# A new instruction order for a fused attention and bilinear kernel, from a search with three smaller constants in its model

## The chip, the cores and the metric

The kernel runs on one core of a Trainium2 chip. The metric is the device time of one execution in microseconds. A core has five engines with a queue of instructions each: TensorE (PE in the profile, with its weight loads as PEld), VectorE (DVE), ScalarE (ACT), GpSimd (POOL) and SyncE (SP), which here only starts DMA transfers. Matmuls write to PSUM, eight banks of 128 partitions by 512 fp32 values; the other engines read the banks and write to SBUF. Engines are ordered among each other by semaphores alone; inside one engine the order of the program holds.

## The reference

One input `x` of 2048 tokens by 512 feeds two branches, which a gate per token mixes. `A` is a multi-head attention with 32 heads of 16, without a mask; `B` is a bilinear unit of width 1376.

```python
qkv = (x @ wqkv).reshape(B, S, 3, H, Dh).transpose(2, 0, 3, 1, 4)
scores = einsum("bhqd,bhkd->bhqk", q, k) * Dh ** -0.5
a = merge_heads(softmax(scores) @ v) @ wo
b = ((x @ w_gate) * (x @ w_up)) @ w_down
g = sigmoid((x * gate_w).sum(-1))
out = g * a + (1 - g) * b
```

All tensors are bf16.

## The kernel before

**Work.** The tokens are cut into four chunks of 512 queries and 16 tiles of 128 keys; the heads into four blocks of eight, of which four pairs lie side by side on the partitions and two parities follow each other. That makes 32 groups (chunk, block, parity), and a group has 16 x 4 score units: one unit is the scores of one head for 128 keys by 512 queries, one PSUM bank. There are 2,048 units.

**TensorE has two tilings.** In the row tiling the array is four tiles of 32 rows, and one burst computes up to four units, one for each head of the four, each into a bank of its own (`burst`, the matmul in L910). In the column tiling it is four tiles of 32 columns, and one pack of four matmuls adds probabilities times values for four heads into the one output bank (`pv_pack`, L1143), or does one 128-deep piece of a projection, of the bilinear unit or of the output (`mm_col`, L427, called by `run_fill`). A piece of the output tile may also be cut into quarters of 32 rows, one of which rides along in a burst (`mm_row`, L433).

**The exponentials** are shared by two engines. ScalarE takes one, two or three neighbouring banks with one instruction (`act_step`, L1008). VectorE computes a base value for one bank by integer arithmetic on the bits (`dve_exp`, L1043), and GpSimd derives two shifted copies of it (`pool_step`, L1093); three packs with differently scaled values then replace one. `more` gives VectorE 20 or 24 of a group's 64 units. The rest of VectorE's work is the evacuation of projections, the bilinear products, the softmax's denominators and the output.

**What sets the order.** The kernel is planned when it is built. `_Clock` keeps a model time for each engine; `issue` notes when an operation begins, when its engine is free again (`dur`) and when its result can be used (`lat`, and 55 ns more for a semaphore, `SEM`). At each model time every free engine is asked for its next step: `pe_step` lists the candidates (a burst `b`, a burst with other shares `x` or `y`, a burst into banks that are about to be free `l`, a pack `p`, a fill `f`, waiting `w`), `act_step` chooses among three, two and one banks, `dve_step` between an evacuation and an exponential. Wherever there is more than one candidate, `choose` reads the next digit of the string `ORDER` as the index into the list. The string thus fixes the whole program; it has 3,094 digits, one for each such decision, and 2,690 of them are 0, the first candidate. The string is the outcome of a search outside of the kernel, which isn't part of it.

The constants of the model that matter here are `MM` (a pack or burst, 216 ns), `SWITCH` (added where the tiling changes, in `pe_issue`), `SECOND` (added to the step behind), `AHEAD` and `LATER` (how long before a bank is free a step in the other tiling may be planned into it) and the `dur` and `lat` of each instruction. None of them is an operand of an instruction. What the plan emits are the instructions in each engine's order, with semaphore waits for the true dependences alone: a constant that is too short can't break a dependence, it only puts an instruction at a place where it will wait.

Of the kernel before, what the change touches and what calls it, by code (L numbers as in the profile page):

```python
# [203 lines left out]
def bass_gated_mix__mha_block__glu_gated_bilinear__prompt_kernel(  # L204
# [12 lines left out]


ORDER = (
    "0000000000000011000001000001000001000000010001000001000000500000000000000000000000001000001010501000"  # L220
    "0000100000000000000000000010001000010000010000000000100000000000000100001000010200000000200010000003"
    "0000000000000040000100000000002002000000000100101000000100010000011100000000000000000000100001000000"
    "5000000020000000200100000010000000000000010000302000000002000000000020020400000000000000100000010000"
    "2000202000012000000000000000000002100000000001000100000000000000020030010030010000000000000022000020"
    "0001000000000001000000000040000000000002210000000000000030010000000000000000001000011000000001000000"
    "0002100000010000000100040000000100000010100000001000000000200000002020000000010000000000200001010000"
    "1005000000000000010000400000010000000000000003000000000000000030100000000010000010000000000000000010"
    "0300000100000000100000000104000000000000000200000002000000000100000000000000000000000010000100000130"
    "3101004000010000100000000000000000000010020000000000000000000000000103030002000100000010000000000000"
    "0000000000000000021000000013030000000000001000011000002200000001100020000000000000002000000002000000"  # L230
    "0200000000200001000200003000000000000000000000020000001000000000000400010002000000000400000020000000"
    "0000000040000000000020000000200000002001200000000000010000000002002000002000000000000000002020100002"
    "0000000040000000100301000000000000000000000100000310010000000000002000000000000101000000000000000000"
    "0200000002000000000100000050000200000010000000003001000000000003002000000000050000000100020000003000"
    "0000000001000010030000010000010010000000020000000011000000000011000000000000000020002200000012000000"
    "0000100000000011050000004000000010000000000001011000200000000000000001000000000000000000000000000000"
    "0000010000000100000000000000000000002110000000000100000000401020000004001000000010000000000000000000"
    "0000101000020004000100000000000000002000010000000311000100000033000000000020030000001000000000040000"
    "0100000000010000100000000000100200000000101000200000000000000000010100000000000000200001000100000100"
    "4110000002000000005000004001000000010000000000000000300000020000000200000010000000010001100040000000"  # L240
    "0000010000000100000000000001000000000000000020000000200000000010000000001100000000000000000000100020"
    "0000000000000000001000000001001005000000300000000000001000000001000000000001000000000000000000000000"
    "0000020000000010001000000000000000000010000000500000000000000000000000000000000000001000010000000002"
    "0000000001000000002000200000002000000000000300000011000100000000000000000200020000020000000000000000"
    "0000000000000202000030000010050010300000001000000000020001000000000000000100002000000000000000000002"
    "0000000200000002001000000001000000010000000000000000011020000010000010000000000000001000000000020100"
    "0000200000000000000000101000000000001000000000001000000000000000200200100000002000000020000001000000"
    "0000010000020001000000010001003000000200000001100000000004000000000000000000000000000100000000000000"
    "0020020000000000000000000000000010000220000000000000000000000020000001200000200000000200500000000100"
    "0000000100050000001040001000300001004010020002011002020000200110000000000000000000000000000000"  # L250
)
HOOK, STOP = None, [1e9]
S, D, H, Dh, F = 2048, 512, 32, 16, 1376
# [6 lines left out]
VR = (203 / 256, 161 / 256)  # L260
NC, NPOOL = 58, 7
OB = 7
MM, SWITCH, SECOND, MML, AHEAD, LATER = 216.0, 108.0, 10.0, 390.0, 90.0, 150.0


class _Tile:
# [23 lines left out]
def _build(nc, A_x, A_wqkv, A_wo, W_gate, W_up, W_down, gate_w, out):  # L290
# [8 lines left out]
    with ExitStack() as stack:  # L299
# [479 lines left out]
        pt_free, pt_rel = list(range(NC)), {i: [] for i in range(NC)}  # L779
        pt_rel[0] = pt_first  # L780
        y_out = [0]
        pool_add = deque()
# [190 lines left out]
        def span2(lo, n, step):  # L973
            return slice(lo, lo + (n - 1) * step + 1, step)

        def act_step():
            if K.pick("act", 1):
                return True
            n = min(len(act_ready), len(pt_free) - 2 * y_out[0])
            if n < 0:  # L980
                n = 0
            if not n:
                return K.pick("act")
            us = [act_ready[0]]
            if n > 1:
                near = [x for x in act_ready if abs(x[1] - us[0][1]) == 1]
                at = {x[1] - us[0][1]: x for x in act_ready}
                three = next(([at[a], at[b]] for a, b in ((1, 2), (1, -1), (-1, -2)) if a in at and b in at), None) if n > 2 and len(pt_free) - 2 * y_out[0] >= 10 else None
                how = choose("a", (["3"] if three else []) + ["2", "1"]) if near else "1"
                if how == "3":  # L990
                    us += three
                elif how == "2":
                    us.append(three[0] if three else near[0])
                us.sort(key=lambda x: x[1])
            n = len(us)
            for x in us:
                act_ready.remove(x)
            if n == 3:
                cells = next([a, b, c_] for k1, b in enumerate(pt_free) for a in pt_free for c_ in (2 * b - a,) if a < b and c_ in pt_free)
                for q in cells:  # L1000
                    pt_free.remove(q)
            else:
                cells = sorted(pt_free.pop(0) for _ in range(n))
            banks = [x[1] for x in us]
            deps = [x[2] for x in us] + [o for q in cells for o in pt_rel[q]]
            bs = slice(banks[0], banks[0] + n)
            cs = span2(cells[0], n, cells[1] - cells[0] if n > 1 else 1)
            o = K.issue("act", lambda a: a.activation(PT[:, cs, :], ps[:, bs, :], ACT.Exp, scale=math.log(2.0) / 1024.0),  # L1008
                        deps, 63.0 + 427.0 * n, 176.0 + 427.0 * n)
            soon(o, banks)  # L1010
            act_out[0] -= n
            o.work = 452.0 * n
            for (u, bank, _), q in zip(us, cells):
                m, kt, j = u

                def free(last, q=q):
                    pt_rel[q] = [last]
                    pt_free.append(q)
                put(_PV(m, j, kt, 0, PT[:, q, :], o, free))
            return True  # L1020

        def put(it):
            pvq.setdefault((it.m, it.j), []).append(it)
# [12 lines left out]
        def dve_exp():  # L1036
            if not can_dve():
                return False
            u, bank, dep = dve_ready.popleft()
            by_dve.add(u)  # L1040
            y = pt_free.pop(0)
            y_out[0] += 1
            o = K.issue("dve", lambda v: v.tensor_scalar(PT[:, y, :].bitcast(I16), ps[:, bank, :], BIAS16, 0.0, ALU.add, ALU.max),  # L1043
                        [dep] + pt_rel[y], 600.0, 690.0, lambda o: pool_add.append((u, y, o)))
            soon(o, [bank])
            dve_out[0] -= 1
            o.work = 452.0
            m, kt, j = u
            used = []

            def free(last):
                used.append(last)
                if len(used) == 2:
                    pt_rel[y] = used
                    pt_free.append(y)
            put(_PV(m, j, kt, 0, PT[:, y, :].bitcast(F16), o, free))
            frees[y] = free
            return True
# [402 lines left out]
        def choose(kind, opt):  # L1461

            if len(opt) == 1:
                return opt[0]
            if HOOK is not None:
                return HOOK(kind, opt, K)
            i = n_choice[0]
            n_choice[0] += 1
            return opt[int(ORDER[i])] if i < len(ORDER) and int(ORDER[i]) < len(opt) else opt[0]
# [169 lines left out]
```

## Time and profile before

| | us |
|---|---|
| median of 3 runs | 647.2 |
| lowest and highest | 646.39, 649.96 |
| profiled execution | 646.02 |
| its span, first to last instruction | 644.1 |
| granted TensorE clock, share of full | 0.999 |

The profiled execution's time is 1.9 us longer than the span of its instructions. In the profile's groups a row reads: line, engine, operation, output and inputs, shapes, count, then the busy time in us and the mean of one instruction in ns, then the engine's idle time ahead of the group and what ended it. The busy time of a group is the union of its instructions' time, so four matmuls that run side by side count once. The rows themselves stand in the prediction.

| group | instructions | busy us |
|---|---|---|
| ScalarE's exponentials, L1008 | 743 | 615.5 |
| VectorE's exponentials, L1043 | 728 | 471.9 |
| GpSimd's copies, L1093 | 1,420 | 550.5 |

### The profile page before, as it was taken

The numbers are of one execution on the slowest core, as the hardware profiler recorded it, in microseconds if no ns is written. First come the engines' busy times: TensorE is split into PE (matmuls) and PEld (weight loads), VectorE is DVE, ScalarE is ACT, GpSimd is POOL, SyncE is SP. The second block draws the span as 40 slices with busy tenths as digits, with TensorE's granted clock in tenths as the row PEclk, the third lists the DMA queues.
The fourth block names the chain that finished last, engine by engine and source line by source line (L and its number), as shares of the span: only waits on it lengthen the run. The fifth ranks groups of instructions, "written<-read, shape, count | busy, mean of one in ns | idle before, by whom it ended". The sixth has DMA issues, their size and how long they took to land.

```text
span 644.1 us, 21192 instructions
## 1 busy us (share of the span) xinstructions
PE 636.3 (99%) x8729; PEld 191.4 (30%) x8729; DVE 602.0 (93%) x1020; ACT 621.8 (97%) x754; POOL 553.4 (86%) x1431
## 2 busy tenths in 40 slices
PE   8999999999999999999999999999999999999997
PEld 3332322222223222223232222332322222222333
DVE  6999999999999999999998999999998999999985
ACT  5899999999999999999999999999999999999992
POOL 2669899999999999898889999888897999889881
PEclk9999999999999999999999999999999999999999
DMA  7940201000010100101010010100001010000001
GB/s 151 262 126 16 66 10 40 2 15 24 5 34 10 40 14 16 32 1 36 4 31 16 16 40 11 32 7 21 19 6 40 19 35 3 9 23 1 28 20 36
DMA packets 28659, 21.16 MB, mean 33 GB/s; under 512 B 16488, under 2 KB 24396, under 8 KB 28560
## 3 DMA queue, kind: packets, MB, share of 16 engines
q1 hardware_dynamic: 27744, 19.40, 11.5%
q8 instruction: 68, 1.11, 0.7%
q10 hardware_dynamic: 816, 0.39, 0.2%
q14 instruction: 31, 0.25, 0.2%
HBM read 11.63 MB, written 2.37 MB: 22 GB/s over the span
## 4 chain that ended last, share of the span: by engine, by line
PE 89%; ACT 9%; DMA 1%; SPq 0%; issue 0%
PE ps L1143 32%; PE ps L427 28%; PE ps L910 26%; ACT PT L1008 9%; PE ps L433 3%; DMA wq<-in_A_wqkv_dram 1%; ACT QE L712 0%; PE ps L1254 0%; SPq L354 0%
## 5 line engine op out<-in xcount | busy, mean ns | idle before, releaser
L1008 ACT ACTIVATE PT<-ps 128x1024 bf16<-128x1024 f32 (+2 forms) x743 | 615.5, 1007 | 5.1 <-PE ps L910 4.5
L1093 POOL INT64_ADD PT<-PT x1420 | 550.5, 408 | 74.6 <-DVE PT L1043 65.2
L1043 DVE TENSOR_SCALAR PT<-ps 128x512 int16<-128x512 f32 x728 | 471.9, 683 | 27.2 <-PE ps L910 15.5
L910 PE MATMUL ps<-QE,KK 32*128 32x512 bf16 x2048 | 244.7, 384 | 0.1
L1143 PE MATMUL ps<-PT,V 128*32 128x512 bf16 (+1 forms) x2048 | 232.5, 384 | 0.0
L1143 PE MATMUL ps<-PT,VS 128*32 128x512 f16 x1456 | 186.6, 383 | 0.0
L910 PEld LDWEIGHTS ps<-QE,KK 32*128 32x128 bf16 x2048 | 63.4, 91 | 229.9 <-ACT PT L1008 185.4
L1143 PEld LDWEIGHTS ps<-PT,V 128*32 128x32 bf16 x2048 | 57.7, 95 | 62.9 <-issue 49.4
L1143 PEld LDWEIGHTS ps<-PT,VS 128*32 128x32 bf16 x1456 | 45.5, 95 | 42.0 <-issue 27.0
L427 PE MATMUL ps<-xT,wg 128*32 128x512 bf16 x704 | 54.6, 383 | 0.0
L427 PE MATMUL ps<-xT,wu 128*32 128x512 bf16 x704 | 54.1, 383 | 0.0
L427 PE MATMUL ps<-wd,wa 128*32 128x512 bf16 x704 | 51.6, 382 | 0.0
L624 DVE TENSOR_TENSOR usb<-ps,omg 128x512 bf16<-128x512 f32 x44 | 30.0, 681 | 0.2
L651 DVE TENSOR_TENSOR wa<-ps,usb 128x512 bf16<-128x512 f32 x44 | 29.9, 680 | 0.1
L433 PE MATMUL ps<-wo,OT 32*128 32x512 bf16 x60 | 23.1, 384 | 0.2
L1240 DVE COPY oc<-ps 128x512 f32<-128x512 f32 x31 | 21.1, 680 | 0.0
L427 PEld LDWEIGHTS ps<-wd,wa 128*32 128x32 bf16 x704 | 14.8, 95 | 19.5 <-issue 11.9
L427 PE MATMUL ps<-xT,wa 128*32 128x512 bf16 x272 | 20.2, 382 | 0.0
L427 PE MATMUL ps<-xT,wq 128*32 128x512 bf16 x256 | 18.5, 382 | 1.4 <-DMA wq<-in_A_wqkv_dram 1.4
L427 PEld LDWEIGHTS ps<-xT,wg 128*32 128x32 bf16 x704 | 13.9, 95 | 18.6 <-issue 11.1
L427 PEld LDWEIGHTS ps<-xT,wu 128*32 128x32 bf16 x704 | 13.7, 95 | 19.0 <-issue 10.4
L427 PE MATMUL ps<-wa,xT 128*32 128x512 bf16 x256 | 17.1, 381 | 0.0
(73 smaller groups left out, 140.9 us busy)
## 6 DMA issues: line engine op xcount, KB each, us to landing
rb<-rscr SPq DMA_DIRECT2D x16, 256.0 KB
QE<-Qr SPq DMA_DIRECT2D x120, 16.0 KB, 1.8
oc<-oc SPq DMA_DIRECT2D x60, 32.0 KB, 1.9
out_dram<-ost SPq DMA_DIRECT2D x12, 128.0 KB, 1.7
wu<-in_B_w_up_dram SPq DMA_DIRECT2D x1, 1376.0 KB, 7.1
wg<-in_B_w_gate_dram SPq DMA_DIRECT2D x1, 1376.0 KB, 11.5
wd<-in_B_w_down_dram SPq DMA_DIRECT2D x1, 1280.0 KB, 14.8
wa<-in_A_wqkv_dram SPq DMA_DIRECT2D x1, 512.0 KB, 5.7
```

The costliest lines, as they stand in the source:

```text
L427: r = pe.matmul(ps[32 * i : 32 * i + 32, bank, :], w, x_, start=s0, stop=s1, tile_position=(0, 32 * i), skip_group_check=True)
L433: return pe.matmul(ps[:, bank, :], lhs[32 * q : 32 * q + 32, :], rhs[32 * q : 32 * q + 32, :], start=s0, stop=s1, tile_position=(32 * q, 0 ...
L624: return v.tensor_tensor(usb[:, st["s"], :], ps[:, bank, :], omg[:, cf, :], ALU.mult)
L651: return v.tensor_tensor(hT[:, f, :], ps[:, bank, :], usb[:, u_at[cf, f][0], :], ALU.mult)
L910: return lambda pe: pe.matmul(ps[:, bank, :], KK[32 * j : 32 * j + 32, b, kt * 128 : (kt + 1) * 128], QE[32 * j : 32 * j + 32, p, b, :], s ...
L1008: o = K.issue("act", lambda a: a.activation(PT[:, cs, :], ps[:, bs, :], ACT.Exp, scale=math.log(2.0) / 1024.0), deps, 63.0 + 427.0 * n, 17 ...
L1043: o = K.issue("dve", lambda v: v.tensor_scalar(PT[:, y, :].bitcast(I16), ps[:, bank, :], BIAS16, 0.0, ALU.add, ALU.max), [dep] + pt_rel[y] ...
L1093: return g.int64_add(PT[:, zl, :].bitcast(I64), PT[:, sl, :].bitcast(I64), w)
L1143: return lambda pe: pe.matmul(ps[32 * it.j : 32 * it.j + 32, OB, :], lhs, it.rhs, start=s0, stop=s1, tile_position=(0, 32 * it.j), skip_gr ...
L1240: K.task("dve", deps, lambda v: v.tensor_copy(oc[:, p, :], ps[:, OB, :]), 600.0, 690.0, done, 0)
```

## The change

Three constants of the planner's model become smaller: the cost of a tiling change from 108 to 106 ns, the delay of a ScalarE exponential from 176 + 427 n to 170 + 427 n ns (n banks), and the delay of a VectorE exponential from 690 to 684 ns. `ORDER` is replaced by another string, found by the search with these constants and another seed. It has 3,108 digits, of which 2,695 are 0, and differs from the first digits on. No function gets other code.

```diff
 ORDER = (
-    "0000000000000011000001000001000001000000010001000001000000500000000000000000000000001000001010501000"
...
-    "0000000100050000001040001000300001004010020002011002020000200110000000000000000000000000000000"
+    "1100000001000000010000000000000001000010000001001032000000011000003000000002000020000000000110000001"
...
+    "0000001020120011022010001000001002440000200000010100020000020000001010100001000011111110000011000000"
+    "00000000"
 )
...
-MM, SWITCH, SECOND, MML, AHEAD, LATER = 216.0, 108.0, 10.0, 390.0, 90.0, 150.0
+MM, SWITCH, SECOND, MML, AHEAD, LATER = 216.0, 106.0, 10.0, 390.0, 90.0, 150.0
...
             o = K.issue("act", lambda a: a.activation(PT[:, cs, :], ps[:, bs, :], ACT.Exp, scale=math.log(2.0) / 1024.0),
-                        deps, 63.0 + 427.0 * n, 176.0 + 427.0 * n)
+                        deps, 63.0 + 427.0 * n, 170.0 + 427.0 * n)
...
             o = K.issue("dve", lambda v: v.tensor_scalar(PT[:, y, :].bitcast(I16), ps[:, bank, :], BIAS16, 0.0, ALU.add, ALU.max),
-                        [dep] + pt_rel[y], 600.0, 690.0, lambda o: pool_add.append((u, y, o)))
+                        [dep] + pt_rel[y], 600.0, 684.0, lambda o: pool_add.append((u, y, o)))
```

More of the change, by code (lines that the diff above doesn't have):

```diff
@@ L219 @@
 ORDER = (
-    "0000000000000011000001000001000001000000010001000001000000500000000000000000000000001000001010501000"
[L221 to L249, printed above, removed]
@@ L250 @@
-    "0000000100050000001040001000300001004010020002011002020000200110000000000000000000000000000000"
+    "1100000001000000010000000000000001000010000001001032000000011000003000000002000020000000000110000001"
+    "0000000200001001000001000000100000000100003001100000000000100000000000010000100000000300000000001000"
+    "0100000000000002000001000000000000020401000000000000000100000000000000010101000000100000000010003300"
+    "0000000000001000200000100000000000000000111000300120000300000000000010000000010000030000000200000000"
@@ new lines @@
+    "0002000000002020000000000000000000000000000000000000000000000000001000000000001000000001000000000020"
+    "0010000000000000110000000000200001000200100000010000000500000020000100000200000100000010000000001000"
+    "0000000000010200000000000000100000002000040000000021000000001000000000001100000000100000000000000000"
+    "0000023300001000100001000000000000000110000100020000000200020000000200000000010000000101000000000002"
+    "0010000000000000000010000110000000000010000002000000000000000000000000100000100000000000000010003000"
@@ new lines @@
+    "3000000000000000004000000010100000101400000000500000000500000000401000000000000000000000100000000010"
+    "0040200000004000003010000300000000000000000000000000003010000000000000000000000000004000000000000000"
+    "0020000000000000000000000000000000010000100000000000000000000000000500103032000000000000011000100000"
+    "0000000000000010000000010000000000000000002000000110000000000000000000020000000000020000002000000020"
+    "0000000400000000001000000500000000401011000011200001102000000050001000000102000000000020000000040000"
@@ new lines @@
+    "0020000000200000000010000000100000000000000000100000000000000000000100000000000020000000200000001000"
+    "0000000010000000010000030000010000000010000000000000000000010000000000010100000000000000001000100010"
+    "0200000020000000000000000000200000000000100000102100000001110000100211403000000100001000400000000002"
+    "1000010000130300000020000000100000000000000000000010000000010000001000005000000020000000000000010000"
+    "0100000000000000002000000000000100002000300100000000010040000000000010040000000100200000000011005001"
@@ new lines @@
+    "0000020000002000100000000100000000000000002000100000000000001000000010000000001000020000004000000000"
+    "0000000001000002002000000000000200100122000100100000000000200000001000010000000100000100000000100000"
+    "0000000004000000100000000000000400000000000200000002000000000100000001000002000000001000001540001010"
+    "0000000000001000000001000000000000000000000000020000010004021005000000000200001000000000000000050000"
+    "0000000000010000000100000000200000000002000000000000000000000000000000000140000100000000000000000000"
@@ new lines @@
+    "2000000050000000001000000000000000000000000000000020002000000000000400000100000000000000000000000000"
+    "0000002000000000000000000000000140002000000000010000000000000000000000010003000000010200000010000000"
+    "0100000000000002000000020000000000000011020000100001000000000000001000010000000010000000010000000000"
+    "0000000000000000210001000000000001000004000000000000000004002000100000000000001010000000000002000000"
+    "0002000004000000100000000100000001000000400000010050000001000000000000000000000000020000000200000000"
@@ L251 @@
+    "0110000001000000030000010000000100000100011000210000000103010500000000010020000004000020010000003000"
+    "0000001020120011022010001000001002440000200000010100020000020000001010100001000011111110000011000000"
+    "00000000"
 )
```

## The prediction

> **What bounds the kernel now.** I read the page first: the busy shares and the chain of work that ended last.
>
> ```profile
> span 644.1 us, 21192 instructions
> PE 636.3 (99%) x8729; PEld 191.4 (30%) x8729; DVE 602.0 (93%) x1020; ACT 621.8 (97%) x754; POOL 553.4 (86%) x1431
> PE 89%; ACT 9%; DMA 1%; SPq 0%; issue 0%
> L1008 ACT ACTIVATE PT<-ps 128x1024 bf16<-128x1024 f32 (+2 forms) x743 | 615.5, 1007 | 5.1 <-PE ps L910 4.5
> L1043 DVE TENSOR_SCALAR PT<-ps 128x512 int16<-128x512 f32 x728 | 471.9, 683 | 27.2 <-PE ps L910 15.5
> L910 PE MATMUL ps<-QE,KK 32*128 32x512 bf16 x2048 | 244.7, 384 | 0.1
> L433 PE MATMUL ps<-wo,OT 32*128 32x512 bf16 x60 | 23.1, 384 | 0.2
> ```
>
> TensorE is busy for 99% of the span and makes 89% of the chain, but ScalarE is nearly as full: in front of its 743 exponentials it idles 5.1 us in all. Next I read the busy time by stage (PE, PEld, DVE, ACT and POOL in this order).
>
> ```profile
> 100.00:200.00 100.00, 100.00 (x1340) 29.27 (x1340) 97.68 (x162) 100.00 (x118) 92.36 (x239) 1.00 0.07 19
> 200.00:300.00 100.00, 99.85 (x1366) 28.96 (x1366) 94.32 (x156) 99.53 (x121) 92.42 (x239) 1.00 0.08 23
> 300.00:400.00 100.00, 100.00 (x1387) 29.02 (x1379) 94.12 (x152) 99.95 (x120) 89.90 (x232) 1.00 0.07 20
> 400.00:500.00 100.00, 100.00 (x1379) 29.49 (x1375) 94.52 (x154) 99.92 (x122) 87.61 (x229) 1.00 0.07 20
> 500.00:550.00 50.00, 49.99 (x692) 14.62 (x692) 47.62 (x78) 49.92 (x60) 46.66 (x119) 1.00 0.06 18
> 629.50:644.10 14.60, 9.98 (x163) 4.46 (x155) 6.88 (x19) 3.41 (x7) 1.44 (x4) 0.95 0.12 39
> ```
>
> From 100 to 550 us TensorE lacks 0.16 us and ScalarE 0.68 us of 450: two engines are full at once, at a granted clock of 1.00. There is no idle stretch that a better order could close; it can only make TensorE's or ScalarE's work smaller. What of TensorE's work an order can change is seen in the chain, piece by piece (start, length, matmuls in the piece).
>
> ```profile
> 90.35 0.33 PE ps L910 x4
> 90.68 1.19 PE ps L427 x20
> 91.87 0.33 PE ps L910 x4
> 92.20 0.76 PE ps L1143 x12
> 92.96 0.33 PE ps L910 x4
> 93.29 0.76 PE ps L1143 x12
> 94.05 0.32 PE ps L910 x3
> 94.37 0.55 PE ps L1143 x8
> 94.92 0.33 PE ps L910 x4
> ```
>
> L910 is the row tiling (a burst of up to four score units); L427 and L1143 are the column tiling (packs of four matmuls). Two packs take 0.55 us, three 0.76, five 1.19: a pack more is (1.19 - 0.55) / 3 = 0.213, say 0.215 us. A burst of three or four takes 0.32 to 0.33 us, and so does the last pack ahead of a burst (0.55 - 0.215 = 0.335). A tiling change therefore adds some 0.11 us, with 0.005 of rounding. A burst with the change into it and the change out of it costs 0.215 + 2 x 0.11 = 0.44 us, whether it carries three units or four: this is the number that an order trades in.
>
> How many bursts there are is read from what the weight loader waited for.
>
> ```profile
> PEld ps L910 <- ACT PT L1008: 185.4, 443, 0.5
> PEld ps L910 <- DVE PT L1043: 23.4, 58, 0.4
> PEld ps L433 <- PE ps L910: 13.6, 35, 0.4
> PEld ps L910 <- issue: 11.7, 31, 0.4
> PEld ps L433 <- issue: 9.3, 22, 0.4
> PEld ps L910 <- DVE V L555: 3.0, 7, 0.4
> ```
>
> These six rows hold 596 entries into the row tiling, of some 0.4 us each; small rows bring it to about 614. So 2,048 score units go out in 614 bursts, 3.34 a burst, with 1,228 changes. The sum against the span: (8,729 - 2,048 - 60) / 4 = 1,655 column packs at 0.215 make 356; 614 bursts at 0.215 make 132; 1,228 changes at 0.11 make 135; together 623 us. The ends come from the chain:
>
> ```profile
> 1.67 4.89 DMA wq<-in_A_wqkv_dram
> 6.70 2.99 PE ps L427 x52
> 633.59 5.54 PE ps L427 x100
> 639.15 1.09 ACT QE L712 x2
> ```
>
> 6.7 us lie before the first projection and 5.0 behind 639.15. That gives 635 of 644.1; the 9 us left are within the rounding (0.005 us on some 3,500 steps could be 17). A fifth of the span is tiling changes.
>
> **The change, part by part.** The profiled execution took 646.0 us for its span of 644.1, so 1.9 us lie around the span; the median of the runs shown is 647.2, another 1.2 above. I work in differences and add them to 647.2.
>
> *The constant for a tiling change, 108 to 106.* No instruction reads it. By the rows a change is 0.105 to 0.115 us, so neither value can be told from the other here. Its direct price is 0. In the plan it takes 2 ns off 1,228 changes, 2.5 us of the plan's own bookkeeping, so a burst of three is a shade cheaper against waiting for a fourth bank.
>
> *The exponentials' delays, 176 to 170 and 690 to 684.* Also bookkeeping alone. The rows for them, by form:
>
> ```profile
> L1008 ACT ACTIVATE PT<-ps 128x1024 bf16<-128x1024 f32 x525 | 501.0, 1107 | 1.0 <-PE ps L910 0.6
> L1008 ACT ACTIVATE PT<-ps 128x512 bf16<-128x512 f32 x192 | 114.6, 666 | 2.0 <-PE ps L910 1.8
> L1008 ACT ACTIVATE PT<-ps 128x1536 bf16<-128x1536 f32 x26 | 39.3, 1510 | 2.1 <-PE ps L910 2.1
> ```
>
> With the 55 ns that the plan adds for a signal, it held a two-bank exponential to release its bank after 1,085 ns and now says 1,079; the row has 1,107. VectorE's was 690 and becomes 684 (without the signal), with 683 in the row. So one moves 6 ns away from its row and the other 6 ns toward it. If every entry into the row tiling that a ScalarE or VectorE exponential released (443 + 58 rows) came 6 ns too early and stood there, TensorE would lose 501 x 6 ns = 3.0 us; if the releases lie inside the change itself, 0. The 443 waits average 185.4 / 443 = 0.42 us and the longest is 0.5: they are nearly all of one length, that of the change, so the release is seldom what comes last. I take 0 and keep 3.0 for the range.
>
> [...]
>
> *The new order.* This is all that the chip sees. The instructions are nearly the same ones: the score matmuls, the projections, and the bilinear branch don't depend on it. What can differ:
>
> - The number of bursts, at 0.44 us each. Both strings hold one digit for each decision that had more than one candidate: 3,094 before, 3,108 after. Every burst, pack and fill of TensorE is such a decision; so are its waits, and many choices of ScalarE between one, two and three banks. If all 14 more were bursts, the price is 14 x 0.44 = 6.2 us; if the growth is in waits and single banks, and better filled bursts go with it, it is below nothing. Twelve bursts fewer (3.40 units a burst) would be worth 5.3 us.
> - The share that VectorE takes, 20 or 24 units of a group of 64: 728 = 22 x 24 + 10 x 20. One group moved takes 4 x 501.0 / (2 x 525) = 1.9 us from ScalarE and adds 4 x 471.9 / 728 = 2.6 us to VectorE and two packs (0.43 us) to TensorE. ScalarE is full, so fewer bursts pay in full only if two or three groups move too; without that the gain ends at the 5.1 us that ScalarE idles.
> - The tail: 25 column packs in 5.54 us behind 633.59. Ten more or fewer left there are 10 x 0.215 = 2.2 us either way; I take 0.
> - Transfers: queues keep their kinds and sizes, and the DMA share is 0.06 to 0.08 in the steady stages, so moved issues have room; 0, with no row that asks for more.
>
> The bounds of the order are thus -5.3 and +6.2 us. Between them the trace decides little; both orders are searched for the same two full engines. I take a third of the 2.5 us that the plan no longer charges for changes as the worth of its better weighing: -0.8 us. The sum is 647.2 - 0.8 = 646.4 us, that is, no change that a measurement can tell. The bound of what can be told is 0.5% (3.2 us, 644.0 to 650.4); the three runs shown are themselves 3.6 us apart.
>
> **The rivals.**
>
> *Fuller bursts (faster).* The order packs 3.40 units a burst instead of 3.34 and moves two or three groups to VectorE, which is 93% busy and has 42 us left. 602 bursts: -5.3 us at most, 641.9; with ScalarE's limit some 642.5. For it: the mean of 3.34 leaves room below four, and L910's 31 entries that waited for nothing show that banks are at times there early. Against it: from 100 to 550 us ScalarE has 0.68 us to give.
>
> *More bursts (slower).* With changes priced lower, the plan goes out with three units, or two, where it waited before; the 14 more decisions are bursts. Its place is between 16 and 629 us, its price 0.44 us each, and it decides from 8 bursts on (3.5 us). Fourteen give 653.4, eight 650.7. For it: the longer string. Against it: decisions of other kinds are four fifths of the string.
>
> *Too early an entry (slower).* The plan is 28 ns short of the ScalarE row where it was 22 short; TensorE then stands at L910. 501 x 6 ns = 3.0 us: 650.2. Against it: the even length of the 443 waits. [...]
>
> *The change does nothing of its own:* the order is another one of the same worth, the time is 647.2; this is counted with the forecast.
>
> **How the numbers follow.** Forecast 0.55, fuller bursts 0.25, more bursts 0.14, early entry 0.06. The forecast's own range is the tail's and its own 2.2 us around 646.4: 644.2 to 648.6. To hold 8 in 10 the range takes in the faster rival's 642.5 and the early entry's 650.2 and leaves out most of the more-bursts case: 642.5 to 650.4. Faster by over 0.5%: 0.25 and 0.02 from the forecast's edge, 0.27. Slower: 0.14 and half of 0.06, and 0.01 of the edge, 0.18. Within 0.5%: 0.55.
>
> **What would show it.** In the waits of the profile after, the entries of the weight loader into L910 and L433 count the bursts: 606 to 622 fits the forecast, under 604 the first rival, 622 and more the second. Early entry would show as a mean of the ScalarE waits above 0.42 us with a longest one above 0.5, and TensorE short of 450 us between 100 and 550. A pack and a burst should still be 0.215 and 0.33 us. The exponentials should still be about 743 and VectorE's 728 give or take 8. The forecast is wrong if the burst count stays and the time leaves 644.0 to 650.4: then the tail, or ScalarE's count, has done it.

## The result, and the profile after

| | before | changed |
|---|---|---|
| median, lowest and highest of 6 runs, us | 646.29 (645.69 to 649.96) | 650.39 (649.77 to 652.26) |
| ratio, 95% interval | | 1.0061 (1.0041 to 1.0081) |
| profiled execution, us | 646.02 | 649.77 |
| its span, us | 644.1 | 646.8 |
| around the span, us | 1.9 | 3.0 |

The changed kernel is slower by 4.1 us, 0.6%. Not all of it lies inside the span: in its six runs 2.8 to 3.2 us lie around it (median 3.1), where 43 runs of the kernel before, taken beside experiments 1 to 8, have 1.5 to 2.0 (median 1.7). The median span of the six is 647.4; of the 20 runs of before on the chip of experiments 1 to 4 it is 644.6. So some 1.4 us came behind or ahead of the instructions, and 2.8 us among them.

The page after:

```profile
span 646.8 us, 21220 instructions
PE 637.6 (99%) x8729; PEld 189.5 (29%) x8729; DVE 605.9 (94%) x1020; ACT 621.9 (96%) x747; POOL 552.2 (85%) x1417
PE 94%; DVE 3%; DMA 1%; SPq 1%; issue 1%; ACT 0%; DVEq 0%
L1009 ACT ACTIVATE PT<-ps 128x1024 bf16<-128x1024 f32 (+2 forms) x736 | 615.5, 1000 | 8.8 <-PE ps L911 7.7
L1044 DVE TENSOR_SCALAR PT<-ps 128x512 int16<-128x512 f32 x728 | 471.8, 683 | 26.5 <-PE ps L911 13.1
L911 PE MATMUL ps<-QE,KK 32*128 32x512 bf16 x2048 | 246.9, 384 | 1.8 <-DVE PT L1044 1.7
```

(Lines are one further down than before.) VectorE's share is the same 728 units, and ScalarE has seven instructions less, with the same busy time. New are three things: VectorE stands in the chain with 3%, TensorE idles 1.7 us in front of a score burst for a VectorE exponential (0.1 us of any kind before), and ScalarE idles 3.7 us more. The stages from 100 to 550 us say where:

```profile
100.00:200.00 100.00, 99.24 (x1337) 28.09 (x1329) 96.89 (x158) 99.00 (x112) 88.16 (x225) 1.00 0.07 19
200.00:300.00 100.00, 99.92 (x1376) 28.72 (x1368) 95.11 (x156) 99.64 (x119) 92.87 (x239) 1.00 0.08 23
300.00:400.00 100.00, 98.83 (x1356) 28.91 (x1352) 94.78 (x151) 97.52 (x123) 89.18 (x231) 1.00 0.07 20
400.00:500.00 100.00, 100.00 (x1377) 29.25 (x1374) 94.59 (x156) 99.42 (x122) 88.36 (x226) 1.00 0.07 20
500.00:550.00 50.00, 50.00 (x705) 14.49 (x706) 47.12 (x77) 49.82 (x60) 44.50 (x115) 1.00 0.07 19
```

TensorE lacks 2.0 us of 450 (before 0.16), nearly all of it between 100 and 200 and between 300 and 400. The weight loader's waits:

```profile
PEld ps L911 <- ACT PT L1009: 188.8, 452, 0.5
PEld ps L911 <- DVE PT L1044: 26.7, 61, 1.2
PEld ps L434 <- PE ps L911: 16.9, 41, 0.4
PEld ps L911 <- issue: 12.1, 31, 0.4
PEld ps L434 <- issue: 8.1, 19, 0.4
PE ps L911 <- DVE PT L1044: 1.7, 2, 0.9
```

These rows and the small ones hold 623 entries where before had 614; counted change by change, from the starts of the matmuls, it is 616 against 612. ScalarE's waits average 188.8 / 452 = 0.42 us with a longest of 0.5, as before. What is different is VectorE's longest, 1.2 instead of 0.4. What held VectorE up is seen in the group that multiplies the attention output by the reciprocals, `OT` from `oc` and `rb`, first before, then after:

```profile
L1222 DVE TENSOR_TENSOR OT<-oc,rb 128x512 bf16<-128x512 f32 x15 | 11.5, 765 | 0.0
```

```profile
L1223 DVE TENSOR_TENSOR OT<-oc,rb 128x512 bf16<-128x512 f32 x15 | 15.3, 1021 | 0.3 <-DMA rb<-rscr 0.3
```

The same 15 instructions take 3.8 us more. Twelve of them take 0.68 to 0.98 us; numbers 4, 8 and 9 take 2.05, 1.45 and 2.18. The timeline around the fourth (start, length, then engine and group):

```profile
185.68 6.78 POOL L1094 INT64_ADD PT<-PT  x18
...
190.95 2.05 DVE L1223 TENSOR_TENSOR OT<-oc,rb 128x512 bf16<-128x512 f32 x1
...
192.92 0.68 DVE L1044 TENSOR_SCALAR PT<-ps 128x512 int16<-128x512 f32 x1
...
193.66 0.39 PE L911 MATMUL ps<-QE,KK 32*128 32x512 bf16 x1 [0.76 <-DVE PT L1044]
193.70 0.77 POOL L1094 INT64_ADD PT<-PT  x2 [1.24 <-DVE PT L1044]
```

GpSimd's stream of 18 additions runs to 185.68 + 6.78 = 192.46, and the multiply ends at 193.00, 0.54 us behind it. Numbers 8 and 9 also end 0.54 us behind the end of a stream. The exponential behind the multiply is late, so its bank is, so the burst is: TensorE stands 0.94 us there, 0.31 and 1.07 us at the other two (starts of the matmuls against the usual distance). In the kernel before, the fourth multiply lies in a stream too and is let in:

```profile
184.95 4.78 POOL L1093 INT64_ADD PT<-PT  x11
...
185.36 1.89 DVE L1043 TENSOR_SCALAR PT<-ps 128x512 int16<-128x512 f32 x3
...
187.17 0.81 DVE L1222 TENSOR_TENSOR OT<-oc,rb 128x512 bf16<-128x512 f32 x1
```

Two theories were put to the chip. **The port** (a name for what the two engines would share; no run shows the thing itself): VectorE's multiply reads two tensors in SBUF and has to get past GpSimd's additions; in the new order it does not get in at three places. **The end of the program:** the 1.4 us around the span have a cause of their own. Their rivals: reciprocals that land late, more bursts, chance from run to run.

### The profile page after: what moved, and what is told of

The parts are those of the page before. It is cut to its first block, busy times and chain, and to the rows that moved or that the text cites. A ratio compares the mean times of both kernels' runs of the same rounds, so it can differ in the third digit from the quotient of the medians.

```text
span 646.8 us, 21220 instructions
## 1 busy us (share of the span) xinstructions
PE 637.6 (99%) x8729; PEld 189.5 (29%) x8729; DVE 605.9 (94%) x1020; ACT 621.9 (96%) x747; POOL 552.2 (85%) x1417
## 4 chain that ended last, share of the span: by engine, by line
PE 94%; DVE 3%; DMA 1%; SPq 1%; issue 1%; ACT 0%; DVEq 0%
PE ps L1144 34%; PE ps L428 29%; PE ps L911 28%; PE ps L434 3%; DVE PT L1044 1%; DVE OT L1223 1%; DMA rb<-rscr 1%; DMA PT<-in_A_x_dram 0%; SPq L525 0%; DVE oc L1241 0%; SPq L1197 0%; ACT xT L476 0%; PE ps L1255 0%; PE ps L466 0%; SPq L1229 0%
## 5 line engine op out<-in xcount | busy, mean ns | idle before, releaser
L1144 PE MATMUL ps<-PT,V 128*32 128x512 bf16 (+1 forms) x2048 | 230.1, 384 | 0.4 <-DVE oc L1241 0.4
L911 PEld LDWEIGHTS ps<-QE,KK 32*128 32x128 bf16 x2048 | 63.3, 90 | 234.8 <-ACT PT L1009 188.8
L1144 PEld LDWEIGHTS ps<-PT,V 128*32 128x32 bf16 x2048 | 56.2, 95 | 61.1 <-issue 49.2
L428 PE MATMUL ps<-xT,wu 128*32 128x512 bf16 x704 | 53.5, 383 | 0.0
L428 PE MATMUL ps<-xT,wg 128*32 128x512 bf16 x704 | 53.3, 382 | 0.0
L428 PE MATMUL ps<-wd,wa 128*32 128x512 bf16 x704 | 51.7, 382 | 0.0
L434 PE MATMUL ps<-wo,OT 32*128 32x512 bf16 x64 | 24.6, 384 | 0.2
L428 PEld LDWEIGHTS ps<-wd,wa 128*32 128x32 bf16 x704 | 14.8, 95 | 19.3 <-issue 12.1
L428 PE MATMUL ps<-xT,wq 128*32 128x512 bf16 x256 | 19.8, 383 | 0.6 <-ACT xT L476 0.6
L428 PE MATMUL ps<-xT,wa 128*32 128x512 bf16 x272 | 20.3, 382 | 0.0
L428 PEld LDWEIGHTS ps<-xT,wu 128*32 128x32 bf16 x704 | 13.9, 95 | 18.4 <-issue 10.0
L428 PEld LDWEIGHTS ps<-xT,wg 128*32 128x32 bf16 x704 | 13.9, 95 | 17.5 <-issue 10.0
L428 PE MATMUL ps<-wa,xT 128*32 128x512 bf16 x256 | 16.7, 381 | 0.0
```

The costliest lines, as they stand in the source:

```text
L428: r = pe.matmul(ps[32 * i : 32 * i + 32, bank, :], w, x_, start=s0, stop=s1, tile_position=(0, 32 * i), skip_group_check=True)
L434: return pe.matmul(ps[:, bank, :], lhs[32 * q : 32 * q + 32, :], rhs[32 * q : 32 * q + 32, :], start=s0, stop=s1, tile_position=(32 * q, 0 ...
L911: return lambda pe: pe.matmul(ps[:, bank, :], KK[32 * j : 32 * j + 32, b, kt * 128 : (kt + 1) * 128], QE[32 * j : 32 * j + 32, p, b, :], s ...
L1144: return lambda pe: pe.matmul(ps[32 * it.j : 32 * it.j + 32, OB, :], lhs, it.rhs, start=s0, stop=s1, tile_position=(0, 32 * it.j), skip_gr ...
```

## The experiments

**1. GpSimd waits for the multiply (the port).** The first addition that is planned behind each multiply waits for it; the order on each engine stays.

```diff
-mult_done[cb] = o7
+mult_done[cb] = port[0] = o7
...
-o = K.issue("pool", fn, [x[2] for x in us] + [d for z in zs for d in pt_rel[z]], 157.0 + 218.0 * n, 182.0 + 218.0 * n)
+o = K.issue("pool", fn, [x[2] for x in us] + [d for z in zs for d in pt_rel[z]] + port, 157.0 + 218.0 * n, 182.0 + 218.0 * n); port[0] = None
```

> The changed kernel, with one wait more at 15 places: GpSimd's first copy planned behind each multiply of the attention output by the reciprocals (OT from oc and rb) waits for that multiply; the order on every engine stays. Theory (the SBUF port): in the profile after, three of these multiplies took 2.05, 1.45 and 2.18 us because GpSimd's stream of additions held the port that VectorE needs for a second SBUF input, and TensorE then stood 0.94, 0.31 and 1.07 us in front of a burst. With the wait all 15 take 0.68 to 1.05 us, the three stalls go, the span falls from 646.8 by 2 to 3.3 us to about 644, and the time from 650.4 to some 647.5. Rival (the reciprocals land late): the three multiplies stay at 1.4 to 2.2 us, GpSimd now idles as well, and the time is 650 to 653. Rival (more bursts, 616 instead of 612, are the cause): the multiplies get shorter and the time stays within 0.5 us of 650.4.

Measured: 648.3 us, 1.0042 (1.0026 to 1.0057) of before; median span 645.3, 2.1 us less than without the wait (experiment 4, the changed kernel on the same chip, has 647.3 in its one run). The multiplies by themselves (shortest, median, longest, ns), and the fourth with the streams around it:

```profile
L1223 DVE TENSOR_TENSOR OT<-oc,rb x15: 679/745/1364, 77.3 to 609.7; 128x512 bf16<-128x512 f32 x15
```

```profile
188.83 3.76 POOL L1094 INT64_ADD PT<-PT  x10
...
191.87 1.26 DVE L1223 TENSOR_TENSOR OT<-oc,rb 128x512 bf16<-128x512 f32 x1
...
193.06 0.68 DVE L1044 TENSOR_SCALAR PT<-ps 128x512 int16<-128x512 f32 x1
193.31 1.52 POOL L1094 INT64_ADD PT<-PT  x4 [0.72 <-DVE OT L1223]
```

GpSimd now stops at 192.59 and idles 0.72 us for the multiply, which still ends 0.54 us behind the stop. The three take 1.27, 1.07 and 1.36 us: they start one or two additions ahead of the one that waits, so they were shortened and not cured, short of the 1.05 us that was expected. The stalls fell from 0.94, 0.31 and 1.07 to 0.16, none and 0.25 us. Late reciprocals would not have been hurried by a wait on GpSimd, and the burst count is the same: as causes of these 2.1 us both rivals fall. The count can still have a share in the 0.7 us that the span stays above before's 644.6; the section on the prediction comes to that.

**2. The same wait in the kernel before.**

> The kernel before with the same wait. Theory (the SBUF port): its multiplies took 0.67 to 1.03 us and none starved, so there is little to gain: within 0.5 us of before, 645.8 to 646.8. Rival (the wait itself is worth or costs something): more than 1 us away from before.

Measured: 646.16 against 646.26 us, ratio 1.0004 (0.9994 to 1.0015). The wait is worth nothing by itself where no multiply is held up: none of the 15 took over 1.03 us in its profile.

**3 and 4. Both kernels again, unchanged.**

> The kernel before, unchanged, for a second profile. Theory: no multiply over 1.1 us again, GpSimd's single additions near 398 ns, TensorE's longest stall in front of a burst under 0.3 us; span 643.8 to 644.5 with 1.9 us around it. Rival (starving is chance from run to run, not the order): one or more multiplies of 1.4 us and more here too.

> The changed kernel, unchanged, for a second profile. Theory: the same three multiplies (numbers 4, 8 and 9 of 15) or neighbours starve again, 1.4 to 2.2 us, the span is 646.8 to 649, 2.8 to 3.2 us lie around it. Rival (chance): no multiply over 1.1 us, and the span falls to 644.

The kernel before, then the changed one, as above:

```profile
L1222 DVE TENSOR_TENSOR OT<-oc,rb x15: 671/727/1797, 77.0 to 609.7; 128x512 bf16<-128x512 f32 x15
```

```profile
L1223 DVE TENSOR_TENSOR OT<-oc,rb x15: 679/868/2108, 77.1 to 611.7; 128x512 bf16<-128x512 f32 x15
```

In the changed kernel the same three starved (2.02, 1.62 and 2.11 us; 650.39 us). In the kernel before, three others did this time (numbers 3, 5 and 13: 1.66, 1.78 and 1.80), its span was 646.6 and its time 648.2. So the miss: the kernel before is not free of it. In its first profile and in experiment 2 GpSimd's additions overlap by 24 ns (398 long, 374 apart) and none of its multiplies starves, that is, none waits through several additions; in this one they last 400 to 420 and three do. In the changed kernel three starve with additions of 398 as well as with 400 to 420. So the order has a part in where a multiply starves, and how GpSimd runs goes with whether it does. What the new order loses by this depends on it too. From the start of the first burst to the end of the last, one profile each, the kernel before takes 619.5 and the changed one 623.3 us with additions of 398; with the longer ones it is 622.1 and 623.2.

**5 and 6. Empty instructions for SyncE (the end of the program).** In the traces instructions are fetched in pieces of 16 or 8 KB; the kernel before has (queue, packets, MB, share):

```profile
q8 instruction: 68, 1.11, 0.7%
q14 instruction: 31, 0.25, 0.2%
```

These 1.36 MB against its 21,192 recorded instructions make 64 bytes each, an estimated 128 instructions to a piece of 8 KB, the page of the expectations. The last piece of 8 KB (the last page) is fetched 2.1 to 2.4 us behind the last instruction in the changed kernel and 0.1 to 0.2 us behind it in the kernel before; a piece of 16 KB at 0.7 to 1.3 us is in both.

```diff
+            if asked < 0 and len(den_op) >= 16:
+                asked = 0
+                for _ in range(8):
+                    P.op("sp", lambda e: e.nop())
```

> The changed kernel with the 15 waits of the first experiment and eight empty instructions more in SyncE's queue, put there halfway through. Theory (the end of the program): with the new order 3.0 us lie around the span instead of 1.8, because the last page of instructions is fetched 2.2 us behind the last instruction instead of 0.2; where the page ends is decided by the length of SyncE's program (336 instructions against 335). With eight more the last fetch moves back to within 0.3 us of the end, 1.7 to 2.0 us lie around the span, the span stays at 645.3, and the time falls from 648.3 to 647.1. Rival (another engine's program, or the end of the last transfer, sets it): 2.9 to 3.2 us still lie around the span and the time stays at 648.3.

> The kernel before with one empty instruction more in SyncE's queue, put there halfway through. Theory (the end of the program): 335 becomes 336, the last page is fetched 2.2 us behind the last instruction, some 3.0 us lie around the span instead of 1.6 to 1.9, and the time rises by 1.2 us to 647.5. Rival: nothing changes, 646.0 to 646.5.

Both tried nothing: the compiled programs have the length they had, 336 and 335 SyncE instructions in the profile, so the empty ones were dropped. The first is a repeat of experiment 1 (648.72 against 647.54 us for before on that chip, 1.0015). Its median span, 645.65 us, is that of before there, 645.7, so the whole difference lies around the span. The second is a repeat of before, in which the numbers 3, 5 and 13 starved again (1.76, 1.78 and 1.80 us).

**7. The port by itself.** Streams of 30 additions with VectorE products in them, and nothing else.

> No part of the computation: 16 streams of 30 GpSimd additions on one cell each; into each stream VectorE puts two copies out of PSUM, one product and a third copy, at the 5th to the 12th addition. In every other stream the product reads two fp32 tensors in SBUF, in the others one in PSUM and one in SBUF. Theory (the SBUF port, held for as long as additions follow each other without a gap): the product from PSUM takes 0.68 us everywhere; that of two SBUF tensors takes 0.7 to 1.1 us in some streams and in others lasts until the stream ends, up to 9 us. Rival (one addition is waited for, never more): it takes at most 0.68 + 0.4 = 1.1 us everywhere.

```profile
L154 DVE TENSOR_TENSOR OT<-oc,rb 128x512 bf16<-128x512 f32 x8 | 6.4, 797 | 0.0
L157 DVE TENSOR_TENSOR OT<-ps,usb 128x512 bf16<-128x512 f32 x8 | 5.4, 680 | 0.0
```

The product of two SBUF tensors took 0.80 us in each of its eight streams, the one from PSUM 0.68, and only beside the first kind did an addition take 0.83 instead of 0.40 us. So such a product and an addition lengthen each other, but no product starved here. All eight began 143 to 145 ns after the start of an addition, since an addition's signal had released VectorE; the last section returns to that.

**8. One constant with the old string.** `SWITCH` 106 in the kernel before.

> The kernel before with one part of the change alone: 106 instead of 108 for the tiling change, with the old string. Theory (string and constants are one thing): the digits meet other lists of candidates from the first moved decision on, the order is no longer the one that was searched for, with more bursts (about 650) and idle time; the plan's own clock ends near 709 us, and the chip follows it to within 1%: 700 to 716. Rival (a constant of 2 ns alone moves little): 646 to 650.

```profile
span 705.9 us, 20874 instructions
PE 676.9 (96%) x8641; PEld 204.6 (29%) x8641; DVE 582.3 (82%) x976; ACT 652.4 (92%) x778; POOL 530.0 (75%) x1375
```

707.5 us, at a granted clock of 0.98. A constant that no instruction reads costs 60 us when it is changed under a string that was searched with another: the digits then index other lists. So this constant has no effect that can be tried alone, and the change is taken as one new order; the two delays were not tried.

**9 to 11. Which engine's program.** One-column operations behind an engine's last instruction.

```diff
+        for k in range(106):
+            P.op("pool", lambda e, k=k: e.memset(pad[:, k : k + 1], 0.0))
```

> The changed kernel with the 15 waits and 106 one-column memsets behind GpSimd's last instruction, where it is idle, so that its program ends at the same place of a 128-instruction page as before. The eight empty instructions of the experiment on SyncE never reached the chip (the program kept its length), so the page theory was not tried by it. Theory (one engine's program ends badly on its page, and it is GpSimd's): 1.6 to 2.0 us lie around the span instead of 2.9 to 3.2, and the last page is fetched 0.2 us behind the last instruction instead of 2.1 to 2.4. Rival (another engine's program, or none): 2.9 to 3.2 us and 2.1 to 2.4 us as before.

> The same with five one-column activations behind ScalarE's last instruction, so that ScalarE's program has the length that it had before. If it is ScalarE's page: 1.6 to 2.0 us around the span, last fetch 0.2 us behind the end. If not: 2.9 to 3.2 us and 2.1 to 2.4 us.

> The same with 121 one-column memsets behind VectorE's last instruction, so that VectorE's program ends at the same place of a page as before. The memsets, about 0.06 us each, may make the span some us longer; what counts is the time around it. If it is VectorE's page: 1.6 to 2.0 us around the span. If not: 2.9 to 3.2 us.

One run each. GpSimd: 3.0 us around the span; ScalarE: 2.9; the last fetch 2.1 to 2.2 us behind the end. Neither. VectorE's memsets delayed its own last branch to 0.63 us ahead of the end, and 3.7 us lie around the span; that answers nothing.

**12 and 13. SyncE's announcement of the last branch.** The last instruction of each engine is a branch (in the kernel before, SyncE's ends 0.85 us ahead of the end and TensorE's at the end); the kernel announces that of TensorE and SyncE ahead of time (`P.ahead`).

```diff
-        P.ahead = {"pe": 60, "sp": 250}
+        P.ahead = {"pe": 60, "sp": 100}
```

> The changed kernel with the 15 waits, and SyncE's announcement of the last branch 100 operations ahead of its end instead of 250. Theory (in the changed kernel the announcement is lost or falls badly): 1.6 to 2.0 us lie around the span instead of 2.9 to 3.1, SyncE's last branch ends 0.85 to 0.9 us ahead of the last instruction instead of 0.52, the last page is fetched 0.2 us behind the end, and the time falls from 648.3 to 647.1. Rival (not SyncE's branch): 2.9 to 3.2 us, 0.52 us and 2.1 to 2.4 us as they were.

> The kernel before without SyncE's announcement of the last branch. Theory: 2.9 us and more lie around the span instead of 1.6 to 1.9, the last page is fetched some 2 us behind the end. Rival (the announcement is worth nothing): 1.6 to 1.9 us.

Moved, it changed nothing: 3.0 us (median of nine runs). Taken out of the kernel before (one run), it left 3.2 us around the span instead of 1.7, and the last fetch came 2.5 us behind the end. In these two things the changed kernel behaves as if it had no announcement. That is no proof that it lost it: the announcement is itself an instruction, so SyncE's program had 334 here, and its branch still ended 0.92 us ahead of the end, as in the kernel before (0.85), where the changed kernel has 0.53.

**14 and 15. The length of SyncE's program.**

```diff
+                for k in range(4):
+                    P.op("sp", lambda e, k=k: e.dma_start(pad[k : k + 1, :], x2[k : k + 1, 0:128]), (), "dout0", 16)
```

> The changed kernel with the 15 waits and four DMAs of 256 bytes more in SyncE's queue halfway through (their data is used by nothing): SyncE's program has 340 instructions. Theory (the place of the last branch in SyncE's program decides whether the announcement works, and 336 is a bad length): 1.6 to 2.0 us lie around the span, SyncE's branch ends 0.85 to 0.9 us ahead of the end, the last fetch is 0.2 us behind it, the time falls from 648.3 to 647.1. Rival (something else in the new program): 2.9 to 3.2 us.

> The kernel before with one such DMA: 336 instructions. Theory: 2.9 to 3.2 us lie around the span instead of 1.6 to 1.9, SyncE's branch ends 0.52 us ahead of the end, and the time rises by 1.2 us, to 647.5 where before has 646.3. Rival: 1.6 to 1.9 us, the time of before.

With 340 instructions the changed kernel has 1.6 us around its span (12 runs, 1.56 to 1.95), with SyncE's branch ending 0.86 us ahead of the end; the kernel before with 336 has 3.2 (2.96 to 3.38) and 0.58 us, with a median span of 645.75 against 645.8. Its time is 648.99 against 647.39 us, ratio 1.0026 (1.0016 to 1.0035). So the length of SyncE's program decides over these 1.4 us; by which mechanism stays open. Two of the numbers were not met. Before's time rose by 1.6 instead of 1.2 us. The changed kernel's time, 648.49 us, is not below the 648.3 of experiment 1, but this chip is another one, where before takes 647.39 instead of 646.26: against before on the same chip the difference fell from 2.0 to 1.1 us. What is left there lies in the span (646.9 against 645.8), and in its profile three multiplies waited 0.16, 0.66 and 1.24 us for the reciprocals, which come through the queue that the four transfers were put into.

No version here beats the kernel before.

## Why the prediction was wrong

It forecast 646.4 us, 0.8 us less than 647.2 and no change that can be told; measured are 4.1 us more than before, slower by over 0.5%, to which it gave 0.18. The number lies at the very end of its range, and for other reasons than the range had: that it lies inside is luck. The base hides a part of the miss, since six runs of before have 646.3 us where the first three had 647.2: the difference is off by 4.9 us (4.1 more instead of 0.8 less). As what would have done it if the burst count stays, the prediction names the tail or ScalarE's count; it was neither.

- *The constants' direct price, 0:* this stands on the code, in which no instruction reads them; by experiment 8 the first can't be measured alone.
- *A step of 0.215, a change of 0.11, a burst of 0.44 us:* the count of entries stayed in the forecast's 606 to 622 by the trace's changes (616), one above by the waits (623). Four bursts more (616 against 612) are 1.8 us by the prediction's price. Idle time can't show them, since a tiling change counts as busy time in the profile: with the wait of experiment 1, TensorE lacks only 0.4 us of the 450. From the first burst to the end of the last, the kernel before takes 619.5 to 619.7 us where no multiply starves (its first profile, experiments 2 and 13), and the changed kernel with the wait 620.9 to 621.1 (experiments 1, 5, 9, 10 and 12). That is some 1.4 us more, of which 0.4 us are longer gaps between matmuls. About 1 us is left, of the sign and the order of size of the four bursts; no run varied their number alone, so their part is not shown.
- *Early entry:* right at 0. The 452 waits for ScalarE are 0.42 us long on average, none over 0.5. What was late is seen on VectorE instead: the exponential queued behind the fourth multiply began at 192.92 us, 0.08 us ahead of the multiply's end, and TensorE waited for it.
- *The share and ScalarE's work:* right, 728 units as before, and fewer single banks:

```profile
L1009 ACT ACTIVATE PT<-ps 128x1024 bf16<-128x1024 f32 x546 | 517.2, 1093 | 2.5 <-PE ps L911 1.8
L1009 ACT ACTIVATE PT<-ps 128x512 bf16<-128x512 f32 x171 | 99.3, 645 | 3.6 <-PE ps L911 3.3
```

- *The tail:* the row for it, `635.95 6.22 PE ps L428 x112`, has 28 packs instead of 25, 0.6 us, within the 2.2 allowed.
- **The step that failed first** is the sentence "What can differ" under the new order, with its four entries. It held the length of every instruction fixed and let an order change only counts and places. The multiply's length depends on what GpSimd does beside it: 0.77 us on average before, 1.02 after. The profile of before showed it at other numbers, which the prediction doesn't use: the longest of the 15 took 1.03 us where the shortest took 0.67, and the plan's 760 ns has no place for it. It cost 2.3 us of stalls in the profile, and experiment 1 got 2.1 us back.
- **The step that failed second** is "1.9 us lie around the span", carried over as a constant. With one instruction more in SyncE's program it became 3.0 in the profile, and 1.7 became 3.1 in the medians.
- *Left open:* 1.4 and 2.1 us are accounted for of 4.1. The remaining 0.7 us of span was not taken apart by a run. In it are the bursts above, what is left of the long multiplies (0.16 and 0.25 us), and 0.5 us at 617 us, where a pack waits for VectorE's copy of `oc`; what lies behind the last burst is up to 0.5 us shorter than before.
- *The worth of the better weighing, -0.8 us:* no run shows it. The plan's own clock did end earlier, at 642.9 us instead of 644.4; the chip gave nothing of that back. The lower constant alone takes 2.5 us off the plan's 1,228 changes by the prediction's own count, so these 1.4 us don't even show that the order is better in the plan.

## What to carry to other kernels

An order that was searched in a model is only as good as the model. Here TensorE was full but for 0.16 us of 450 in the steady stages, and what the model does not see (a multiply that has to wait for GpSimd, and the end of the program) decided between two orders 0.6% apart. Before an order is judged, look in its trace for the longest instance of each repeated instruction, not the mean, and compare the time around the span apart from the span. A digit string that steers a planner belongs to exactly one set of constants.

## What the runs showed of the hardware that was not expected

**A VectorE product of two SBUF tensors can wait through several GpSimd additions in a row.** In the seventeen profiles with 248 such products, 27 took 1.2 us or more, up to 2.2, and the additions are some 374 ns apart. All 27 began 28 to 64 or 262 to 327 ns after the start of an addition; none of those that began 100 to 222 ns after one took over 0.85 us. Not every one in the bad stretches starves, and what decides there stays open. In experiment 7 an addition beside such a product takes 0.83 us instead of 0.40, beside one from PSUM 0.40. There an addition is lengthened by one product; in the 27 a product is lengthened by up to four additions. The additions last some 398 ns or more at a distance of 374, so that by these records a stream has no moment without one.

**One instruction more in SyncE's program cost 1.4 to 1.6 us at the end.** With 335, 340 and 342 instructions (the last in one run, experiment 8) 1.5 to 2.0 us lie around the span, with 336 it is 2.8 to 3.4, in two different orders; experiment 11, which delayed another engine's branch, is left out. With 334, and without the announcement of the last branch, it is 3.2. Why 336 is a bad length was not tried further.
